# The first layer's weights in eight loads of 256 KB instead of sixteen of 128 KB, and a new order of all work

## The chip, the core and the metric

The kernel runs on one core of one Trainium2 chip. A core has a matrix engine (TensorE, PE in the profile; its weight loads are PEld), a vector engine (VectorE, DVE), a scalar engine (ScalarE, ACT), a general engine (GpSimd, POOL) and a queue engine (SyncE, SP). Each works through its own list of instructions in order; semaphores make one wait for another. DMA engines move data between the chip's main memory and the core's on-chip memory; a transfer is issued by an instruction of GpSimd, SyncE or ScalarE. The metric is the device time of one execution in microseconds (us); lower is better.

## What is computed

Eight batches of two softmax attentions in a row, then a two-layer network with a squared ReLU, all inputs and outputs in float32:

```python
def sm_attn(qq, kk, vv):
    s = scale * np.matmul(qq, kk.transpose(0, 1, 3, 2))
    s = s - np.max(s, axis=-1, keepdims=True)
    a = np.exp(s)
    a = a / (np.sum(a, axis=-1, keepdims=True) + 1e-09)
    return np.matmul(a, vv)
p_packed = sm_attn(p, k, v)
out = sm_attn(q, p_packed, p_packed)
...
h = x @ w_in
r = np.maximum(h, 0.0)
g = r * r
return (g @ w_out).astype(np.float32)
```

There are 8 batches, 8 heads, 576 queries and keys for each, heads of 64, and 32 packed queries p. After the attention the heads stand side by side, so that x has 4608 rows of 512; w_in is 512 x 2048 and w_out 2048 x 512.

## The kernel before

**Stages.** Batch by batch the kernel does the following; the names are those of its own list of work, with the batch as first number. `S1` multiplies packed queries with keys (L733; L749 for batches 5 to 7), `MX` takes the row maximum (L752), `EX` the exponential (L760), `E` turns the result round (L766, or a DMA transpose for batches 5 to 7), `PV` multiplies with the values (L780), `XN` divides by the sum, `XM` and `XC` turn that round (L799). `M` multiplies the result with w_in (L810): as the second attention is linear in its values, w_in is applied to the 32 packed rows of each head before the attention weights are. `MC` casts `M` from the accumulators to on-chip memory (L606 on ScalarE, L608 on VectorE). `S2` multiplies queries with the packed rows (L827, L837), `SI` turns the scores round on VectorE (L848), `SM` takes the maximum (L854), `SU` subtracts it (L858), `SE` is the exponential on ScalarE (L861), `SS` the sum (L864), `SN` divides (L871), `SO` turns the weights round (L875). `F` and `F1` multiply these weights with `M`, which gives the first layer (L912 for batches 0 and 1, L884 later), `R` is the ReLU (L920 and L922, L894 and L896), `Q` and `SQ` the square (L930 and L932, L902 and L904). `F2` is the second layer (L938), partly in groups that save one multiplication in eight (`GP`, L1005, fed by sums and differences `gS` on VectorE, L990). Results go out through L950.

**Batch 0 in thirds.** The first batch is cut into three parts of 128, 192 and 256 tokens, so that the first layer can start early: `F.0.0`, `F.0.1` and `F.0.2`, and `SE.0.0` to `SE.0.2` in the same way. w_in is used in four quarters of 512 columns, `M.0.0` to `M.0.3`; a quarter has to be there as a whole before its `M` is complete.

**Loads.** All loads but the first keys and p are issued by GpSimd (`load`, L1048) in a fixed order, `ORDER`: keys and values of batch 0, a first part of its queries, the first quarter of w_in, the rest of the queries, the other quarters, then keys of batch 1, w_out, and so on. They convert from float32 to bfloat16 on the way. A load waits until the load eight places before it has landed (`issued[-8]`), so at most eight are under way. A quarter of w_in came as four loads: two halves of the embedding (`qd`), each in two pairs of heads (`i`), 128 KB each in bfloat16.

**Order.** No engine's order is written by hand. A planner (`Plan.forward`) goes through time with a cost for each piece of work and picks by a priority: a level by batch and stage, plus a number for each piece from `TABLE`. The table was found by a search. The planner's costs and the landing times that it assumes decide which piece is put first; the program that comes out is fixed, and every engine then follows its list whatever the real times are. Where the planner expects TensorE to be idle for over 0.7 us, it puts in fills (`keep_clock`, L612), matmuls of a zero tile whose result nobody reads.

Of the kernel before, what the change touches and what calls it, by code (L numbers as in the profile page):

```python
# [14 lines left out]
P = 128  # L15
D = 64
# [5 lines left out]
WCH = 512  # L22
# [19 lines left out]
class Plan:  # L42
# [6 lines left out]
    def add(self, *a, **kw):  # L49
        self.pieces.append(Piece(*a, **kw))  # L50
# [177 lines left out]
TABLE = {'o': {'Lk.0.0i': -41.988702, 'Lk.0.1i': 172.502158, 'Lk.0.0': 181.505648, 'LP.0': -6.041854, 'Lk.0.1':  # L228
# [289 lines left out]
def kernel_impl(tc, q, k, v, p, w_in, w_out, out):  # L518
    nc = tc.nc
# [22 lines left out]
    with ExitStack() as ctx:  # L542
# [52 lines left out]
        QDS = range(NQD)  # L595
# [800 lines left out]
```

## Time and profile before

| | us |
|---|---|
| median of 3 runs | 235.95 (235.69 to 235.96) |
| profiled execution, its own time | 235.75 |
| its span, first to last instruction | 234.0 |
| TensorE busy | 221.4 (95%) |
| VectorE busy | 198.1 (85%) |
| ScalarE busy | 152.0 (65%) |
| GpSimd busy | 59.9 (26%) |

The granted TensorE clock was 0.995 of full speed over the span. A row of a group reads: line, engine, operation, output and input with their shapes, count, then busy time, mean ns of one, and the idle time of the engine just before them with what ended it. A row of the timeline reads: start and length in us, engine, line, what it is, count, and in brackets the idle time before it with its releaser. In the chain of waits each row is a start, a length and what the time went to. A row of a stretch reads: from and to, length, busy time and count for each engine, granted clock, share of the DMA engines, GB/s. Busy times of matmuls are modelled and overlap, so that eight matmuls of 0.27 us each can take 0.87 us together.

### The profile page before, as it was taken

Reading aid. Unit: us, or ns where it says so; the run is one execution under the profiler, and the core shown is the slowest. Engines: PE = TensorE matmul, PEld = TensorE weight load, DVE = VectorE, ACT = ScalarE, POOL = GpSimd, SP = SyncE. Lnnn points to the kernel's source line nnn. Section 1 sums busy time; section 2 is a strip of 40 time slices with the busy share of each in tenths; the row PEclk is TensorE's granted clock in tenths of the full one; section 3 lists DMA queues with packets and bytes.
Section 4 is the critical chain, followed back from the end, with each engine's and each line's share of the span. In section 5 each row is a group of like instructions: output and inputs, shape, how many; then the busy total and the mean of one; then the engine's idle time right before and its main releaser. Section 6 shows DMA issues by size and latency. Waiting matters only on the chain.

```text
span 234.0 us, 6384 instructions
## 1 busy us (share of the span) xinstructions
PE 221.4 (95%) x2621; PEld 159.9 (68%) x2638; DVE 198.1 (85%) x332; ACT 152.0 (65%) x247; POOL 59.9 (26%) x107
## 2 busy tenths in 40 slices
PE   8878899999999999999999999999999999999991
PEld 5655665346554566678768787877777888888781
DVE  3769887799999988999999789999999999877240
ACT  3333897469875799984999846459985998501100
POOL 9777745233343666620000000000000000000000
PEclk9999999999999999999999999999999999999998
DMA  7999999999999999999788689609710023205316
GB/s 235 179 169 175 195 204 204 204 194 250 240 205 241 227 220 177 174 182 125 175 150 135 134 116 191 140 2 204 134 39 8 4 44 73 65 0 112 70 43 181
DMA packets 46716, 34.06 MB, mean 146 GB/s; under 512 B 25376, under 2 KB 38432, under 8 KB 46688
## 3 DMA queue, kind: packets, MB, share of 16 engines
q0 software_dynamic: 19456, 18.03, 48.8%
q1 hardware_dynamic: 26304, 14.98, 29.8%
q10 hardware_dynamic: 928, 0.66, 0.9%
q8 instruction: 20, 0.33, 0.6%
q14 instruction: 8, 0.07, 0.1%
HBM read 37.22 MB, written 9.44 MB: 199 GB/s over the span
## 4 chain that ended last, share of the span: by engine, by line
PE 77%; DMA 14%; DVE 3%; POOL 1%; issue 1%; SPq 1%; ACT 0%; DVEq 0%; POOLq 0%
PE ps L1005 29%; PE ps L884 20%; PE ps L938 13%; DMA kq_b<-in_q_dram 7%; PE ps L912 5%; PE ps L810 3%; DMA w_in_b<-in_moe_w_in_dram 3%; DMA v_b<-in_v_dram 3%; DMA out_dram<-o_sb 2%; PE ps L956 1%; PE ps L780 1%; PE ps L827 1%; SPq L950 1%; PE ps L733 1%; POOL v_b L621 1%
## 5 line engine op out<-in xcount | busy, mean ns | idle before, releaser
L894 ACT ACTIVATE r_b<-ps 128x576 bf16<-128x576 f32 x92 | 52.8, 662 | 8.5 <-PE ps L884 8.3
L884 PE MATMUL ps<-a,M 128*128 128x288 bf16 x384 | 52.5, 286 | 0.2
L884 PEld LDWEIGHTS <-M 128*128 128x128 bf16 x384 | 37.3, 98 | 11.6 <-DVE a L875 0.2
L938 PE MATMUL ps<-w_out_b,gT 128*128 128x512 bf16 x159 | 41.2, 380 | 1.3 <-issue 0.6
L1005 PEld LDWEIGHTS <-gT 128*128 128x128 bf16 x384 | 36.9, 98 | 7.5 <-issue 2.4
L606 ACT CAST M<-ps 128x1024 bf16<-128x1024 f32 (+1 forms) x33 | 29.8, 940 | 10.9 <-PE ps L810 8.7
L904 DVE TENSOR_TENSOR gT<-r_b 128x1152 bf16<-128x1152 bf16 x40 | 29.3, 745 | 4.0 <-ACT r_b L894 3.7
L606 ACT COPY o_sb<-ps 128x512 f32<-128x512 f32 (+1 forms) x21 | 11.9, 575 | 30.5 <-PE ps L1005 16.6
L950 POOL DMA_DIRECT2D out_dram<-o_sb x2 | 1.1, 570 | 119.2 <-DVE o_sb L1025 117.7
L1005 PEld LDWEIGHTS <-gS 128*128 128x128 bf16 x288 | 27.7, 98 | 5.1 <-issue 1.8
L938 PEld LDWEIGHTS <-gT 128*128 128x128 bf16 x176 | 15.8, 98 | 15.3 <-issue 2.5
L1025 DVE TENSOR_TENSOR o_sb<-o_sb,ps 128x512 f32<-128x512 f32 x30 | 20.3, 676 | 6.5 <-PE ps L1005 5.7
L1005 PE MATMUL ps<-wS,gT 128*128 128x256 bf16 x192 | 23.5, 273 | 0.5 <-DVE o_sb L1025 0.5
L1005 PE MATMUL ps<-w_out_b,gT 128*128 128x256 bf16 x192 | 23.8, 273 | 0.0
L1005 PE MATMUL ps<-wS,gS 128*128 128x256 bf16 x192 | 23.5, 273 | 0.0
L920 ACT ACTIVATE r_b<-ps 128x512 bf16<-128x512 f32 (+2 forms) x25 | 15.7, 664 | 7.7 <-PE ps L912 6.4
L912 PE MATMUL ps<-a,M 128*128 128x256 bf16 (+3 forms) x160 | 18.6, 262 | 1.3 <-DVE M L608 0.8
L912 PEld LDWEIGHTS <-M 128*128 128x128 bf16 x160 | 13.8, 98 | 6.4 <-issue 1.1
L760 ACT ACTIVATE e<-ps,n 128x576 bf16<-128x576 f32 x16 | 11.7, 737 | 7.0 <-DVE n L752 6.8
L612 PE MATMUL ps<-o_sb 128*128 128x256 bf16 x97 | 14.6, 311 | 1.1 <-DVE o_sb L615 1.1
L752 DVE TENSOR_REDUCE n<-ps 128x1 f32<-128x576 f32 x16 | 11.6, 750 | 2.0 <-PE ps L733 1.8
L612 PEld LDWEIGHTS <-o_sb 128*128 128x128 bf16 x97 | 10.2, 111 | 4.4 <-DVE o_sb L615 1.1
(77 smaller groups left out, 316.9 us busy)
## 6 DMA issues: line engine op xcount, KB each, us to landing
out_dram<-o_sb SPq DMA_DIRECT2D x65, 128.0 KB, 3.4
kq_b<-in_k_dram POOLq DMA_DIRECT2D x14, 288.0 KB, 10.9
kq_b<-in_q_dram POOLq DMA_DIRECT2D x10, 288.0 KB, 6.9
w_in_b<-in_moe_w_in_dram POOLq DMA_DIRECT2D x16, 128.0 KB, 6.1
w_out_b<-in_moe_w_out_dram POOLq DMA_DIRECT2D x8, 256.0 KB, 9.4
v_b<-in_v_dram POOLq DMA_DIRECT2D x5, 320.0 KB, 11.4
v_b<-in_v_dram POOLq DMA_DIRECT2D x12, 128.0 KB, 7.7
v_b<-in_v_dram POOLq DMA_DIRECT2D x5, 256.0 KB, 9.8
```

The source lines that it names most:

```text
L606: nc.scalar.copy(dst, src)
L612: nc.tensor.matmul(half(7)[:, :2 * P], lhsT=zero[:, :P], rhs=zero, start=True, stop=True)
L752: nc.vector.tensor_reduce(n1[b % 2][:, qd:qd + 1], ps1[b, qd], axis=AX.XY if b in XBAR else AX.X, op=ALU.max, negate=True)
L760: nc.scalar.activation(e_out(qd) if b in XBAR else e1[:, qd, :S], ps1[b, qd], ACT.Exp, bias=n1[b % 2][:, qd:qd + 1], accum_out=d1[b % 2][: ...
L884: nc.tensor.matmul(t[:, c], lhsT=M[b % 2][:, qd, fb * FB:(fb + 1) * FB], rhs=a2[b % 2][:, qd, c * HALF:(c + 1) * HALF], start=(qd == 0), s ...
L894: nc.scalar.activation(dst, src, ACT.Relu)
L904: eng.tensor_tensor(out=dst, in0=r, in1=r, op=ALU.mult)
L912: nc.tensor.matmul(t[:, c, m * w:(m + 1) * w], lhsT=M[b % 2][:, qd, fb * FB:(fb + 1) * FB], rhs=a2[b % 2][:, qd, o:o + w], start=(qd == 0) ...
L920: nc.scalar.activation(dst, ph["h", b, x, j], ACT.Relu)
L938: nc.tensor.matmul(po[t], lhsT=gT[:, fb, n0:n0 + P], rhs=w_out_b[:, fb, :], start=(fb == 0), stop=(fb == NFB - 1))
L1005: nc.tensor.matmul(pz[g, k][:, i], lhsT=a[:, f, i * P:(i + 1) * P], rhs=w[:, f], start=(k not in ON and h == 0 and f == 0 and i == 0), sto ...
L1025: nc.vector.tensor_tensor(out=oC(g, i, j), in0=oC(g, *src), in1=pz[g, z], op=ALU.add)
```

## The change

A quarter of w_in comes as two loads (one for each half of the embedding, all four heads) instead of four. The order of the bytes in `ORDER` is the same. The planner's figures for these loads are changed to match, it assumes that some of the early loads land 0.8 us later than before, and the table of priorities is replaced as a whole by that of a new search (837 numbers for the order before, 821 after). `M` waits for two loads instead of four. Nothing else is changed; the arithmetic is the same.

```diff
-        def dma_w_in(c, i, qd):
+        def dma_w_in(c, qd):
             src = w_in[:, c * WCH:(c + 1) * WCH].rearrange("(qd h d) f -> qd d h f", qd=NQD, h=QH)
-            nc.gpsimd.dma_start(w_in_b[qd * D:(qd + 1) * D, 2 * i:2 * i + 2, c * WCH:(c + 1) * WCH], src[qd][:, 2 * i:2 * i + 2])
+            nc.gpsimd.dma_start(w_in_b[qd * D:(qd + 1) * D, :, c * WCH:(c + 1) * WCH], src[qd])
...
-            add(name, [("DMA", us, None)], [f"{name}i"], line="dma", lag=0.9, level=-200)
+            late = 0.8 * (name[:3] == "LWO" or name.split(".")[:2] in (["LWI", "1"], ["LWI", "2"], ["LWI", "3"]) or name[:2] != "LW" and name.split(".")[1] in "12")
+            add(name, [("DMA", us, None)], [f"{name}i"], line="dma", lag=0.9 + late, level=-200)
...
-                for i in range(2):
-                    for qd in QDS:
-                        load(f"LWI.{n}.{i}.{qd}", 0.7 + 0.45 * ((n, i, qd) in ((1, 0, 0), (3, 0, 0), (3, 1, 1))), lambda n=n, i=i, qd=qd: dma_w_in(n, i, qd), 0.6)
+                for qd in QDS:
+                    load(f"LWI.{n}.{qd}", 1.35, lambda n=n, qd=qd: dma_w_in(n, qd), 0.73)
...
-                add(f"M.{b}.{c}", [("PE", 0.216, lambda u, b=b, c=c: m_mm(b, c, u))], [f"XC.{b}"] + [f"LWI.{c}.{i}.{qd}" for i in range(2) for qd in QDS]
+                add(f"M.{b}.{c}", [("PE", 0.216, lambda u, b=b, c=c: m_mm(b, c, u))], [f"XC.{b}"] + [f"LWI.{c}.{qd}" for qd in QDS]
```

What this does to the engines' lists: GpSimd has 100 instructions instead of 107 in the listing. TensorE has 98 fills instead of 97, and the same matmuls otherwise. In the third quarter's turn ScalarE's list now has `SE.0.2` ahead of the two casts of `M.0.2`; before it stood between them. Two pieces of `F.0.2` stand behind batch 1's `S1` instead of ahead of it. The scores `S1.7` of the last batch stand closer behind `S1.6`. The ends of the lists, from the last pieces of the first layer on, differ little.

More of the change, by code (lines that the diff above doesn't have):

```diff
@@ L226 @@
 XTURN = (5, 6, 7)
-TABLE = {'o': {'Lk.0.0i': -41.988702, 'Lk.0.1i': 172.502158, 'Lk.0.0': 181.505648, 'LP.0': -6.041854, 'Lk.0.1':
[287 rows of a table removed]
+TABLE = {'o': {'Lk.0.0i': -1.867589, 'Lk.0.1i': 4.847526, 'Lk.0.0': 27.298004, 'LP.0': 2.29922, 'Lk.0.1': 26.572586,
[282 rows of a table added]
 def kernel_impl(tc, q, k, v, p, w_in, w_out, out):
```

569 rows, old and new, of the table TABLE are left out of this document.

## The prediction

> **What bounds the kernel now.** I read the page first, then the busy time in stretches, then the chain of waits, then the first 33 us instruction by instruction.
>
> ```profile
> PE 221.4 (95%) x2621; PEld 159.9 (68%) x2638; DVE 198.1 (85%) x332; ACT 152.0 (65%) x247; POOL 59.9 (26%) x107
> ```
>
> TensorE is the busy engine. Cut at the first scores of batch 1 (31.90) and the last matmul (229.2), columns PE, PEld, DVE, ACT, POOL:
>
> ```profile
> 0.00:31.90 31.90, 26.49 (x333) 18.80 (x334) 22.83 (x56) 15.54 (x28) 23.94 (x45) 1.00 1.11 192
> 31.90:229.20 197.30, 194.96 (x2288) 141.14 (x2304) 175.30 (x277) 136.14 (x220) 35.86 (x63) 1.00 0.76 138
> ```
>
> ```profile
> L612 PE MATMUL ps<-o_sb 128*128 128x256 bf16 x97 | 14.6, 311 | 1.1 <-DVE o_sb L615 1.1
> ```
>
> After 31.90 TensorE idles 197.30 - 194.96 = 2.3 us. A new order can win at most that there, and lose more. The first stretch is different: all 97 fills of L612, matmuls that compute nothing, lie in its 26.5 us, and 31.90 - 26.49 = 5.4 us are idle. What the change is worth is decided before batch 1 starts. The chain of waits in that stretch runs through loads:
>
> ```profile
> 11.07 5.45 DMA kq_b<-in_q_dram
> 16.81 6.82 DMA w_in_b<-in_moe_w_in_dram
> ```
>
> The second is the last load of the third quarter of w_in (M.0.2 needs it), issued only when the queries of the first had landed. TensorE, ScalarE and VectorE around it:
>
> ```profile
> 22.52 0.40 PE L810 MATMUL ps<-w_in_b,ppT 64*32 64x512 bf16 x5
> 23.67 0.39 PE L810 MATMUL ps<-w_in_b,ppT 64*32 64x512 bf16 x3 [0.74 <-DMA w_in_b<-in_moe_w_in_dram]
> 24.99 2.14 PE L912 MATMUL ps<-a,M 128*128 128x192 bf16 x24
> 27.67 1.06 PE L912 MATMUL ps<-a,M 128*128 128x256 bf16 x8 [0.20 <-DVE a L875]
> 31.90 0.71 PE L733 MATMUL ps<-kT,pT 32*32 32x512 bf16 x32 [0.22 <-DVE r_b L922]
> ```
>
> ```profile
> 22.63 0.60 ACT L920 ACTIVATE r_b<-ps 128x512 bf16<-128x512 f32 x1 [1.09 <-PE ps L912]
> 24.10 0.59 ACT L606 CAST M<-ps 128x512 bf16<-128x512 f32 x1 [0.87 <-PE ps L810]
> 24.58 0.63 ACT L861 ACTIVATE e<-s 128x512 bf16<-128x512 f32 x1
> ```
>
> ```profile
> 16.62 0.65 DVE L697 STREAM_TRANSPOSE qT<-kq_b 128x448 f32<-128x448 f32 x1 [0.64 <-DMA kq_b<-in_q_dram]
> 22.56 0.63 DVE L858 TENSOR_TENSOR s<-s,m 128x512 f32<-128x512 f32 x1
> 23.97 0.37 DVE L875 STREAM_TRANSPOSE a<-n 128x192 f32<-128x192 f32 x1
> 25.25 0.69 DVE L864 TENSOR_REDUCE t<-e 128x16 f32<-128x512 bf16 x1 [0.91 <-ACT e L861]
> 27.17 0.45 DVE L875 STREAM_TRANSPOSE a<-n 128x256 f32<-128x256 f32 x1
> 27.54 0.98 DVE L932 TENSOR_TENSOR gT<-r_b 128x768 bf16<-128x768 bf16 x2
> 29.73 0.85 DVE L932 TENSOR_TENSOR gT<-r_b 128x512 bf16<-128x512 bf16 x2
> 31.20 0.65 DVE L922 TENSOR_SCALAR r_b<-ps 128x512 bf16<-128x512 f32 x1
> ```
>
> See how one late load travels: M.0.2 stands 0.74; its cast stands in ScalarE's queue ahead of the exponential of the last third of batch 0 (SE.0.2); that exponential's input was ready at 22.56 + 0.63 = 23.19, yet it starts at 24.58; VectorE then stands 0.91, and F.0.2, the last third of the first layer, opens at 27.67.
>
> **The change part by part.** Loads first.
>
> ```profile
> L688 POOL DMA_DIRECT2D w_in_b<-in_moe_w_in_dram x16 | 9.5, 622 | 2.5 <-DMA kq_b<-in_q_dram 1.0 <-DMA w_in_b<-in_moe_w_in_dram 0.7 <-DMA v_b<-in_v_dram 0.6
> L691 POOL DMA_DIRECT2D w_out_b<-in_moe_w_out_dram x8 | 5.7, 713 | 4.8 <-DMA w_out_b<-in_moe_w_out_dram 1.8 <-DMA v_b<-in_v_dram 1.6 <-DMA w_in_b<-in_moe_w_in_dram 1.2
> ```
>
> A 256 KB load of w_in has no row; L691 is one of that size and 2 KB pieces, so I take 713 ns. GpSimd saves 16 x 0.622 - 8 x 0.713 = 4.2 us of issuing. By itself this is worth 0: POOL is 26% busy and waits for landings. If the issue cost a full 2 x 0.622, nothing is saved, which is still 0.
>
> What moves the path is the window: a load waits for the one eight loads before it.
>
> ```profile
> 5.42 1.82 POOL L688 DMA_DIRECT2D w_in_b<-in_moe_w_in_dram  x3
> 9.98 0.58 POOL L654 DMA_DIRECT2D kq_b<-in_q_dram  x1 [1.02 <-DMA v_b<-in_v_dram]
> 11.57 4.21 POOL L688 DMA_DIRECT2D w_in_b<-in_moe_w_in_dram  x7
> 16.81 0.58 POOL L688 DMA_DIRECT2D w_in_b<-in_moe_w_in_dram  x1 [1.02 <-DMA kq_b<-in_q_dram]
> ```
>
> ```profile
> w_in_b<-in_moe_w_in_dram POOLq DMA_DIRECT2D x16, 128.0 KB, 6.1
> ```
>
> Eight loads of double size are more bytes in flight. In the new order the last load of the third quarter waits for the first load of the first quarter, whose second half was issued at 5.42 + 0.61 and lands about 6.1 later, at 12.1; so it is issued near 12.7 in place of 16.81. When it lands is then set by bytes. Behind the last piece of the queries (11.07 + 5.45 = 16.52) stand two quarters, 4 x 256 KB = 1.05 MB, at the rates of
>
> ```profile
> 18.00:24.00 6.00, 4.62 (x54) 3.01 (x52) 5.96 (x17) 2.09 (x4) 4.24 (x8) 1.00 1.17 173
> 24.00:30.00 6.00, 5.35 (x60) 4.44 (x58) 4.89 (x12) 5.71 (x10) 4.37 (x7) 1.00 1.17 200
> ```
>
> 173 to 200 GB/s: 5.2 to 6.1 us, so 21.7 to 22.6. The bounds are 21.7 and 23.63 (16.81 + 6.82, no gain, if one slow DMA engine and not the window set it). I take 22.4, nearer to the bytes, because the old load was issued after GpSimd had stood 1.02 for the window. The wait of 0.74 goes. The keys of batch 1 and w_out are issued earlier too, but stand in the same queue of bytes behind the weights; I give that 0.
>
> Five of M.0.2's eight matmuls ran ahead of the last small load, 0.40 us in all; with large loads they would stand behind it if that still came last. The Trainium skill, "Perfetto Trace Analysis", section "DMA Optimizations", has a rule against this change: splitting DMAs into smaller chunks may let some work start sooner. By that rule the trace agrees for these five, and the sum below would come out 0.4 higher; by the landing times above they wait for nothing.
>
> The order. In the new one SE.0.2 stands ahead of both casts of M.0.2 on ScalarE. It starts when its input and the relu before it are done, at about 23.2 (22.63 + 0.60), 1.4 us earlier than 24.58. VectorE's sum at 25.25 follows by 1.4; the transposition at 23.97, which used to lie in VectorE's idle time, now comes behind that sum and gives back 0.3. The two casts, 0.59 each, now end near 25.0; the F that needs them stands behind ten fills and starts about then, as the F in that place did (24.99). F.0.2 can open at 27.67 - 1.4 + 0.3 = 26.6. From there to S1.1, the first scores of batch 1, it was 31.90 - 27.67 = 4.23, nearly all VectorE work. The new list there has one square of 768 columns less (0.98 / 2), one of 512 less (0.85 / 2) and a relu of 768 columns in place of 512 (half of 0.65 more): 4.23 - 0.49 - 0.42 + 0.33 = 3.65. S1.1 comes at 30.25, so 1.65 earlier. But less is done by then: two pieces of F.0.2, eight matmuls, moved behind S1.1, and one matmul more of F2 ahead of it.
>
> ```profile
> 35.83 0.87 PE ps L912 x8
> 36.70 0.65 PE ps L938 x3
> ```
>
> That is 0.87 - 0.22 = 0.65 us of work still owed. Net 1.65 - 0.65 = 1.0 us. There are 98 fills in place of 97; the extra one lies in idle time, or costs 0.1.
>
> Behind S1.1 the matmuls, stores and the last 56 + 16 of TensorE are the same in kind and number, in another order. The old order lost 2.3 us there; nothing says that the new one loses the same. I take a loss of 0.2, with ends of -1 (under half of the 2.3 idle) and +1.2 (the third rival below).
>
> Sum, against the profiled run of 235.75 (span 234.0 and 1.75 around it): -1.0 + 0.1 + 0.2 = -0.7, 235.05. The median of the runs, 235.95, stands 0.2 above the profiled one, so 235.2 for the median.
>
> **The rivals.**
>
> Queries come earlier too. The first of the three last pieces of q waited for the values (1.02 at 9.98); in the new order it waits for nothing, and the last is issued at about 10.0 in place of 11.07. If they land earlier by the 0.64 that VectorE stands at 16.62, the whole softmax of batch 0 shifts: 235.2 - 0.64 = 234.6. For it: those waits were for the window. Against: the same bytes stand ahead of them.
>
> The loads land as before. Then M.0.2 still ends near 24.0, ten fills (at most 14.6 / 97 = 0.15 each; I take 1.1) follow it in TensorE's order, and the first F that needs its casts starts at 25.1 to 25.7; the fourth quarter and the relus behind it shift by about 0.6 to 0.7, and 0.3 is left of the 1.0: 235.2 + 0.65 = 235.85. The rows from 18 to 30 speak for it: the DMA share is 1.17, so a longer queue may win nothing. This is also the case in which the change in loads does not do what it says.
>
> VectorE is overrun by batches 6 and 7. S1.7 came 149.28 - 134.44 = 14.8 us after S1.6; in the new order 20 matmuls of L884, 32 of L1005 and some 1.2 us of small ones lie between, 2.48 + 3.60 + 1.2 = 7.3 us, so half.
>
> ```profile
> 128.75 2.48 PE ps L884 x20
> 134.44 0.38 PE ps L749 x26
> 135.27 3.60 PE ps L1005 x32
> 149.28 0.38 PE ps L749 x26
> ```
>
> ```profile
> 138.00:144.00 6.00, 5.68 (x9) 1.00 1.09 214
> 144.00:150.00 6.00, 6.00 (x10) 1.00 0.72 160
> ```
>
> ```profile
> L752 DVE TENSOR_REDUCE n<-ps 128x1 f32<-128x576 f32 x16 | 11.6, 750 | 2.0 <-PE ps L733 1.8
> ```
>
> VectorE (the columns are its busy time, the clock, the DMA share, GB/s) is full there: 0.32 us free in 12. Batch 7's two maxima of 0.75 move in, ahead of the differences (gS) that release the groups of L1005: 1.5 - 0.3 = 1.2 us. From the point where VectorE is behind TensorE's stock of released groups, each microsecond is idle TensorE: 235.2 + 1.2 = 236.4, and more with the small work that follows the maxima. Against it: the same work is then missing from 150 on, and TensorE showed no idle in 138 to 150.
>
> **How the numbers follow.** Forecast 0.33, queries earlier 0.17, loads as before 0.22, VectorE overrun 0.28. The likeliest gives 235.2. Its own range is 234.8 to 235.7; for 8 in 10 I reach from 233.9 (queries earlier and 0.7 won behind S1.1) to 236.9 (the overrun, and 0.5 for the small work behind the maxima). About 0.2%, 0.47 us, is what can be told from no change here. Faster by more (below 235.48): 0.27 of the forecast, the queries' 0.17, 0.04 of the third, 0.48 in all. Within 0.2%: 0.06 and 0.18, 0.24. Slower: 0.28.
>
> **What would show it.** Right: the wait of M.0.2 for w_in is gone or under 0.2; SE.0.2 starts near 23.2 and ends ahead of the casts; VectorE's wait of 0.91 is gone; the first L733 of batch 1 starts between 29.8 and 30.8; TensorE's idle time from there to its last matmul is 2 to 3 us. Wrong: M.0.2 waits until 23.6 or later; S1.1 is at 31 or later; or TensorE idles over 4 us behind S1.1, with VectorE named at L1005 between 140 and 165.

## The result, and the profile after

| | before | after |
|---|---|---|
| median of four runs each, us | 235.82 (235.34 to 235.96) | 237.59 (236.8 to 237.8) |
| ratio, 95% interval | | 1.0087 (1.0062 to 1.0113) |
| profiled execution, its own time / span, us | 235.75 / 234.0 | 237.58 / 235.8 |

The changed kernel is 1.8 us slower. That lies outside of the range, and on the other side of the forecast.

The page after: busy time, and the same two stretches as before, cut at the first scores of batch 1 (S1.1), now at 31.19:

```profile
PE 223.3 (95%) x2626; PEld 160.8 (68%) x2639; DVE 202.6 (86%) x336; ACT 150.7 (64%) x243; POOL 55.3 (23%) x99
```

```profile
0.00:31.19 31.19, 26.15 (x327) 18.21 (x328) 22.21 (x54) 15.19 (x27) 19.78 (x38) 0.95 1.14 204
31.19:230.70 199.51, 197.11 (x2300) 142.62 (x2312) 180.38 (x284) 135.11 (x216) 35.36 (x62) 1.00 0.78 135
```

The first stretch is 0.71 us shorter (31.90 - 31.19), the second 2.2 longer (199.51 - 197.30). TensorE's idle time in the second is 199.51 - 197.11 = 2.4 us, as before (2.3). These two numbers can't be compared as they stand, because both traces lack records of matmuls. The second layer's line has 176 weight loads in each kernel, but only 159 matmuls in the trace of before and 163 in that of after; a place where one is missing is drawn as idle. Before:

```profile
L938 PE MATMUL ps<-w_out_b,gT 128*128 128x512 bf16 x159 | 41.2, 380 | 1.3 <-issue 0.6 <-DMA kq_b<-in_q_dram 0.2 <-ACT r_b L920 0.2
L938 PEld LDWEIGHTS <-gT 128*128 128x128 bf16 x176 | 15.8, 98 | 15.3 <-issue 2.5 <-DVE gT L932 0.2
```

Two runs of the experiments below have all their records: bf, the old order with ten more fills in its front, and e0, the kernel after once more. The same stretch (S1.1 to the last matmul) of bf, then of e0:

```profile
31.30:227.98 196.68, 196.67 (x2305) 141.17 (x2304) 175.27 (x277) 136.11 (x219) 35.95 (x63) 1.00 0.78 138
```

```profile
31.18:230.78 199.60, 197.95 (x2313) 142.61 (x2312) 180.38 (x284) 135.17 (x216) 35.82 (x63) 1.00 0.77 135
```

The old order leaves TensorE 0.01 us idle there, the new one 1.65, and all but 0.2 of that waits for VectorE. In the trace of before 0.54 of the 2.3 is a wait (for VectorE, at 218 us), and the rest is missing records. VectorE has 180.38 us of work in the second stretch in place of 175.30.

TensorE, VectorE and ScalarE in the front of the changed kernel:

```profile
14.69 3.18 PE L607 MATMUL ps<-o_sb 128*128 128x256 bf16 x15
17.80 0.59 PE L822 MATMUL ps<-qT,pq 32*32 32x192 bf16 x32
22.72 0.41 PE L805 MATMUL ps<-w_in_b,ppT 64*32 64x512 bf16 x8
31.19 0.70 PE L728 MATMUL ps<-kT,pT 32*32 32x512 bf16 x32
```

```profile
16.77 0.65 DVE L692 STREAM_TRANSPOSE qT<-kq_b 128x448 f32<-128x448 f32 x1 [0.60 <-DMA kq_b<-in_q_dram]
...
26.66 0.45 DVE L870 STREAM_TRANSPOSE a<-n 128x256 f32<-128x256 f32 x1 [0.64 <-PE ps L907]
```

```profile
23.41 0.63 ACT L856 ACTIVATE e<-s 128x512 bf16<-128x512 f32 x1
23.95 1.05 ACT L601 CAST M<-ps 128x512 bf16<-128x512 f32 x2
```

M.0.2 runs its eight matmuls at 22.72 without a wait, and SE.0.2 starts at 23.41 ahead of the two casts. But S1.1 comes only 0.71 us earlier, not 1.65. One reason is S2.0.1, the scores of the second third of batch 0: most of its matmuls start at 17.80, before at 17.31. TensorE, before:

```profile
17.31 0.58 PE L827 MATMUL ps<-qT,pq 32*32 32x192 bf16 x28 [0.72 <-DVE qT L697]
```

The queries that S2.0.1 needs still land late (16.77, before 16.62), although their last piece was issued at 10.21 (before 11.07), and the 15 fills that start at 14.69 run until 17.8, though the transposition of the queries has ended at 16.77 + 0.65 = 17.42. The landings of the queries, before and then after (median us from issue in the last column):

```profile
kq_b<-in_q_dram POOLq DMA_DIRECT2D x1, 224.0 KB, 4.3
kq_b<-in_q_dram POOLq DMA_DIRECT2D x2, 112.0 KB, 4.9
```

```profile
w_in_b<-in_moe_w_in_dram POOLq DMA_DIRECT2D x8, 256.0 KB, 8.1
kq_b<-in_q_dram POOLq DMA_DIRECT2D x1, 224.0 KB, 8.5
kq_b<-in_q_dram POOLq DMA_DIRECT2D x2, 112.0 KB, 6.8
```

The chain of waits, shares by engine, before and then after:

```profile
PE 77%; DMA 14%; DVE 3%; POOL 1%; issue 1%; SPq 1%; ACT 0%; DVEq 0%; POOLq 0%
```

```profile
PE 58%; DVE 21%; DMA 9%; issue 4%; ACT 3%; POOL 2%; SPq 1%; DVEq 0%; ACTq 0%; POOLq 0%
```

VectorE has 21% of it in place of 3%: on the page of after, this is where the loss shows.

**Where the time goes.** To find the places I compared when two kernels have done the same useful work. Each matmul of TensorE's list counts the time from its start to the next one's in back-to-back rows of the profile before (0.2165 us for one of F2, 0.1226 for one of 288 columns, 0.1092 in the groups), a fill counts nothing, and the table gives how much later (+) or earlier (-) than the profiled run before each kernel reaches the sum that the old one had reached at the time on the left. Each column is one execution.

| old kernel's time | after | e0 (after again) | e3 | g41 | h41n | x1 |
|---|---|---|---|---|---|---|
| 32.0 | -0.20 | -0.20 | -1.27 | -0.20 | -1.49 | -1.39 |
| 42.4 | -0.19 | -0.18 | -1.24 | -0.26 | -1.47 | -1.37 |
| 51.0 | -0.84 | -0.85 | -1.90 | -0.54 | -0.39 | -2.03 |
| 59.0 | +0.22 | +0.05 | -1.02 | +0.09 | -0.39 | +0.09 |
| 81.2 | -0.01 | -0.01 | -1.01 | +0.03 | -0.30 | -0.13 |
| 105.9 | +0.98 | +0.98 | -0.07 | +1.02 | -0.30 | +0.73 |
| 142.2 | +1.15 | +1.15 | +0.10 | +1.19 | | +0.90 |
| 150.3 | +1.55 | +1.50 | +0.45 | +1.57 | -0.23 | +1.34 |
| 166.5 | +1.73 | +1.67 | +0.63 | +1.39 | -0.24 | +1.51 |
| 202.9 | +1.72 | +1.68 | +0.60 | +1.36 | -0.24 | +1.45 |

The changed kernel wins 0.2 by 32 us and 0.6 more by 51 (second-layer work done ahead), and then loses 1.06 at 51 to 59, 1.0 at 81 to 106, 0.4 at 142 to 150 and some 0.2 up to 166. The table ends ahead of one more wait, at 218, of 0.54 in before and 0.55 in e0, which other runs of both orders lack or have shorter (bf 0, e3 0.29). TensorE in the first two of these places, after:

```profile
50.54 1.04 PE L907 MATMUL ps<-a,M 128*128 128x256 bf16 x8
...
55.71 0.27 PE L907 MATMUL ps<-a,M 128*128 128x256 bf16 x1
56.27 1.36 PE L907 MATMUL ps<-a,M 128*128 128x256 bf16 x11 [0.29 <-DVE a L870]
...
83.95 1.14 PE L879 MATMUL ps<-a,M 128*128 128x288 bf16 x8 [0.33 <-DVE a L870]
```

The first layer of batch 1 opens at 50.54 as before (50.52); the first matmul of its second part (320 columns) starts at 58.33, before at 57.97. Both waits name L870, the transposition of the attention weights (SO) on VectorE. What VectorE got: relus and squares, before and then after.

```profile
L904 DVE TENSOR_TENSOR gT<-r_b 128x1152 bf16<-128x1152 bf16 x40 | 29.3, 745 | 4.0 <-ACT r_b L894 3.7
L902 ACT ACTIVATE gT<-r_b 128x1152 bf16<-128x1152 bf16 x8 | 9.4, 1179 | 0.2
L896 DVE TENSOR_SCALAR r_b<-ps 128x576 bf16<-128x576 f32 x4 | 3.0, 752 | 0.0
```

```profile
L899 DVE TENSOR_TENSOR gT<-r_b 128x1152 bf16<-128x1152 bf16 x34 | 25.0, 747 | 2.3 <-ACT r_b L889 2.1
L897 ACT ACTIVATE gT<-r_b 128x1152 bf16<-128x1152 bf16 x14 | 16.5, 1176 | 0.1
L891 DVE TENSOR_SCALAR r_b<-ps 128x576 bf16<-128x576 f32 x12 | 8.8, 741 | 1.1 <-PE ps L879 0.7 <-DVE s L853 0.3
```

Eight relus moved to VectorE and six squares away from it.

### The profile page after: what moved, and what is told of

Same layout as the page of the kernel before. It is cut to its first block, busy times and chain, and to the rows that moved or that the text cites. A ratio compares the mean times of both kernels' runs of the same rounds, so it can differ in the third digit from the quotient of the medians.

```text
span 235.8 us, 6385 instructions
## 1 busy us (share of the span) xinstructions
PE 223.3 (95%) x2626; PEld 160.8 (68%) x2639; DVE 202.6 (86%) x336; ACT 150.7 (64%) x243; POOL 55.3 (23%) x99
## 4 chain that ended last, share of the span: by engine, by line
PE 58%; DVE 21%; DMA 9%; issue 4%; ACT 3%; POOL 2%; SPq 1%; DVEq 0%; ACTq 0%; POOLq 0%
PE ps L1000 21%; PE ps L879 17%; PE ps L933 9%; DMA kq_b<-in_k_dram 4%; PE ps L907 4%; DMA w_in_b<-in_moe_w_in_dram 3%; DVE o_sb L1020 2%; DVE gS L985 2%; DVE m L849 2%; PE ps L805 2%; DVE s L853 2%; DMA out_dram<-o_sb 2%; DVE t L859 2%; PE ps L951 1%; DVE gT L899 1%
## 5 line engine op out<-in xcount | busy, mean ns | idle before, releaser
L889 ACT ACTIVATE r_b<-ps 128x576 bf16<-128x576 f32 x84 | 49.4, 662 | 16.1 <-PE ps L879 15.9
L1000 PEld LDWEIGHTS <-gT 128*128 128x128 bf16 x384 | 36.9, 98 | 7.3 <-issue 2.4
L601 ACT COPY o_sb<-ps 128x512 f32<-128x512 f32 (+1 forms) x19 | 10.9, 577 | 32.1 <-PE ps L1000 17.7
L601 ACT CAST M<-ps 128x1024 bf16<-128x1024 f32 (+1 forms) x31 | 27.7, 936 | 5.7 <-PE ps L805 5.7
L933 PEld LDWEIGHTS <-gT 128*128 128x128 bf16 x176 | 16.4, 98 | 15.9 <-issue 1.5
L899 DVE TENSOR_TENSOR gT<-r_b 128x1152 bf16<-128x1152 bf16 x34 | 25.0, 747 | 2.3 <-ACT r_b L889 2.1
L915 ACT ACTIVATE r_b<-ps 128x512 bf16<-128x512 f32 (+2 forms) x23 | 14.4, 653 | 9.1 <-PE ps L907 8.8
L897 ACT ACTIVATE gT<-r_b 128x1152 bf16<-128x1152 bf16 x14 | 16.5, 1176 | 0.1
```

Of the source, the lines that this page charges most:

```text
L601: nc.scalar.copy(dst, src)
L889: nc.scalar.activation(dst, src, ACT.Relu)
L897: nc.scalar.activation(dst, r, ACT.Square)
L899: eng.tensor_tensor(out=dst, in0=r, in1=r, op=ALU.mult)
L915: nc.scalar.activation(dst, ph["h", b, x, j], ACT.Relu)
L933: nc.tensor.matmul(po[t], lhsT=gT[:, fb, n0:n0 + P], rhs=w_out_b[:, fb, :], start=(fb == 0), stop=(fb == NFB - 1))
```

## The experiments

Ratios stand against runs of the kernel before on the same chip, with the 95% interval.

| run | what | median us (runs) | ratio |
|---|---|---|---|
| e0 | after, again | 237.33 (12) | 1.0062 (1.0040 to 1.0084) |
| e1 | old order, large loads | 235.25 (12) | 1.0001 (0.9981 to 1.0021) |
| e2 | new order, small loads | 238.52 (5) | 1.0146 (1.0116 to 1.0176) |
| e3 | after, ten more fills | 236.34 (7) | 1.0059 (1.0035 to 1.0082) |
| e4 | after, two casts early | 237.43 (6) | 1.0100 (1.0070 to 1.0130) |
| e5 | after, relus and squares on their old engines | 238.84 (6) | 1.0146 (1.0115 to 1.0177) |
| e6 | e1, softmax ahead of casts | 234.87 (12) | 0.9978 (0.9956 to 0.9999) |
| e7 | e4, more moved back | 238.05 (6) | 1.0099 (1.0071 to 1.0127) |
| h30 | new order to 30 us, old behind | 236.66 (9; a tenth took 454.6) | 1.0042 (1.0012 to 1.0072) |
| h30f | the same with ten fills | 236.94 (6) | 1.0063 (1.0042 to 1.0084) |
| h41n | new to 41 us, old behind | 236.26 (12) | 1.0028 (1.0006 to 1.0051) |
| h41f | the same with ten fills | 235.82 (12) | 0.9999 (0.9978 to 1.0019) |
| h49 | new to 49 us, old behind | 239.04 (6) | 1.0164 (1.0140 to 1.0188) |
| h82 | new to 82 us, old behind | 238.11 (6) | 1.0105 (1.0077 to 1.0132) |
| g41 | old to 41 us, new behind | 236.85 (10) | 1.0063 (1.0038 to 1.0087) |
| bf | before, ten more fills | 234.95 (12) | 0.9974 (0.9955 to 0.9994) |
| x1 | e3, two waits taken away | 237.71 (6) | 1.0121 (1.0078 to 1.0164) |
| y1 | e6 and bf together | 234.92 (12) | 0.9974 (0.9953 to 0.9994) |

**The loads, and the order.** e1 has the old order with the large loads: the first of each pair of issues brings both pairs of heads, the second nothing.

```diff
-            nc.gpsimd.dma_start(w_in_b[qd * D:(qd + 1) * D, 2 * i:2 * i + 2, c * WCH:(c + 1) * WCH], src[qd][:, 2 * i:2 * i + 2])
+            if i == 0:
+                nc.gpsimd.dma_start(w_in_b[qd * D:(qd + 1) * D, :, c * WCH:(c + 1) * WCH], src[qd])
```

> The old order of all work, with the eight loads of 256 KB in place of the sixteen. Theory A (the loss of 1.8 us comes from the new order, the loads alone help): the last load of the third quarter lands by 23, TensorE's wait of 0.74 ahead of L810 is gone, and nothing behind the first scores of batch 1 changes: 235.2 to 235.8. Theory B (the larger loads themselves cost, by what they push back in the queue of bytes): 236.5 to 237.6, with a DMA named in a wait of TensorE or VectorE that the old kernel does not have.

e2 is the reverse: the new order, each load of 256 KB issued as two of 128.

```diff
-            nc.gpsimd.dma_start(w_in_b[qd * D:(qd + 1) * D, :, c * WCH:(c + 1) * WCH], src[qd])
+            for i in range(2):
+                nc.gpsimd.dma_start(w_in_b[qd * D:(qd + 1) * D, 2 * i:2 * i + 2, c * WCH:(c + 1) * WCH], src[qd][:, 2 * i:2 * i + 2])
```

> The new order of all work, each load of 256 KB issued as two of 128 KB at the same place. Theory A: 237.2 to 238.3, as slow as the changed kernel or slower, and M.0.2 waits for w_in again by up to 0.7. Theory B: 235.5 to 236.2.

The loads alone are worth nothing (1.0001). In e1 M.0.2 runs without a wait too, but the queries come later, so S1.1 is at 31.67. VectorE and TensorE of e1:

```profile
16.97 0.65 DVE L698 STREAM_TRANSPOSE qT<-kq_b 128x448 f32<-128x448 f32 x1 [1.47 <-DMA kq_b<-in_q_dram]
```

```profile
22.88 0.41 PE L811 MATMUL ps<-w_in_b,ppT 64*32 64x512 bf16 x8
```

The order carries the loss, and with small loads it is slower still. There GpSimd builds an identity matrix behind more issues, and TensorE waits for it at 11.20 (after: the same matmuls at 9.19 without a wait). TensorE of e2:

```profile
11.20 0.44 PE L762 MATMUL ps<-ident,e 128*128 128x128 bf16 x5 [1.50 <-POOL ident masks.py:199]
23.71 0.39 PE L806 MATMUL ps<-w_in_b,ppT 64*32 64x512 bf16 x3 [0.55 <-DMA w_in_b<-in_moe_w_in_dram]
```

**The clock.** The profiled run after shows a granted clock of 0.95 in the first stretch: the 15 fills above took 3.18 us, 0.21 each, and S2.0.1 stood behind them. e0 is the same kernel once more; e3 adds ten fills where TensorE idles just before.

```diff
+MORE = {'PV.0': 3, 'XM.0': 4, 'M.0.0': 3}
...
+            seq.append([p, n + MORE.get(p.name, 0)])
```

> The changed kernel as it is, beside the others on one chip: 1.8 us slower than the old one by the record, 1.0 if the 3.4 us at half clock do not come on this chip. The runs with a granted clock of 0.997 or more should be 0.7 to 1.1 faster than those with less.

> The changed kernel with ten more fills between 11.5 and 14.2 us (3 ahead of the values product, 4 ahead of the transposition, 3 ahead of the first quarter of batch 0), where TensorE has its idle time just ahead of the 3.4 us at half clock. Theory C (the half clock follows a stretch of light work, and costs 0.8): the granted clock is 0.997 or more in the runs and the median is 236.6 to 237.0. Rival (the dip comes whatever stands there, or costs nothing on the path): clock 0.993 in most runs and 237.4 to 237.9.

e0's trace has the full clock from 12 to 18 us (1.00, after 0.72), yet S2.0.1 at 17.84, S1.1 at 31.18 and the table's curve as after. So a full clock doesn't take the loss away. The two traces agree in S1.1 for different reasons: in after the slow fills held S2.0.1 by some 0.4, in e0 the queries landed 0.4 later. Nor are e0's runs at a clock of 0.997 or more (237.23 to 237.99) faster than its others, though the expectation had them 0.7 to 1.1 faster. In e3's trace the queries came early and S1.1 at 30.12; its ratio isn't told apart from e0's. VectorE of e0, then of e3:

```profile
17.14 0.65 DVE L692 STREAM_TRANSPOSE qT<-kq_b 128x448 f32<-128x448 f32 x1 [0.83 <-DMA kq_b<-in_q_dram]
```

```profile
16.05 0.63 DVE L710 STREAM_TRANSPOSE qT<-kq_b 128x448 f32<-128x448 f32 x1
```

TensorE of e0, then of e3:

```profile
17.84 0.58 PE L822 MATMUL ps<-qT,pq 32*32 32x192 bf16 x28 [1.36 <-DVE qT L692]
```

```profile
16.73 0.59 PE L840 MATMUL ps<-qT,pq 32*32 32x192 bf16 x32
```

S1.1 comes 13.3 to 13.4 us behind these matmuls in after, e0 and e3, and 14.6 behind them in before.

In the traces of kernels with the large loads the queries land early or late. Early (that transposition at 15.7 to 16.05, no wait) were e3, e5, h30f, h41n and x1; late (16.5 to 17.2) after, e0, e4, e7, h30, h41f, h49, h82, g41, and e1, e6, y1. h41n and h41f differ by ten fills alone, and there the one without is early; in after and e3 it is the one with. Each is one execution, so whether the kernel decides it or the execution stays open too.

**Repairs of the new order.** These edits take the planner's finished list and move pieces ahead of others (`MOVES`: piece, and the one it is put ahead of), or change an engine (`SWAP`). e4 puts the last two quarters of batch 1's `M`, and their casts, back to where the old order had them, at 43 to 48 us.

```diff
+MOVES = [('M.1.2', 'F2.3.10'), ('MC.1.2', 'SE.1.0'), ('M.1.3', 'F2.0.12'), ('MC.1.3', 'FC.2')]
```

> The changed kernel with the third and fourth quarter of batch 1's first-layer weights (M.1.2, M.1.3) and their two casts put back to 43 to 48 us, where the old order had them and ScalarE is idle, in place of 53 to 56.5. Theory D (those two casts, 1.9 us of ScalarE in the stretch where the first layer of batch 1 lives on ScalarE and VectorE, make the loss of 1.3 us between 51 and 60): 236.2 to 236.7. Rival (VectorE paces that stretch, with the softmax of batch 1 and the sums wS, and the casts are beside it): 237.2 to 237.7.

e5 gives 28 relus and squares of batches 2 to 7 the engine that they had before.

```diff
+SWAP = {'R.2.0': 'ACT', 'R.2.6': 'ACT', 'SQ.3.0': 'ACT', 'SQ.3.1': 'DVE',
...
```

> The changed kernel with 28 relus and squares of batches 2 to 7 given back to the engine that had them in the old one (13 relus from VectorE to ScalarE or the other way, 15 squares likewise), in the new order of all work otherwise. A relu of 576 columns takes 0.59 on ScalarE and 0.73 on VectorE, a square of 1152 columns 1.18 on ScalarE and 0.73 on VectorE; the new list has 8 more relus on VectorE and 6 more squares on ScalarE, 3.8 us more work for the same result. Theory W (that is what TensorE waits for behind 80 us, where both engines are full): 0.5 to 1.0 less than the changed kernel run beside it, and VectorE's busy time 199 to 201 in place of 202.6. Rival (the positions in the order decide, not the engine): within 0.3 of it, or slower.

e7 is e4 with `WS.2.1` (sums of w_out on VectorE) and a transposition of batch 2's keys behind `SO.1.0`, and six pieces of F2 spread through the first layer.

```diff
+MOVES = [('M.1.2', 'F2.3.10'), ('MC.1.2', 'SE.1.0'), ('M.1.3', 'F2.0.12'), ('MC.1.3', 'FC.2'), ('F2.1.10', 'F.1.0.2'), ('F2.1.11', 'F.1.0.2'), ('F2.1.12', 'F.1.0.3'), ('F2.1.13', 'F.1.0.3'), ('F2.1.14', 'F2.5.0'), ('F2.1.15', 'F2.5.0'), ('FC.1', 'Q.1.0.3'), ('ST.1', 'Q.1.0.3'), ('WS.2.1', 'Tk.2.1'), ('Tk.2.0', 'Tk.2.1')]
```

> The changed kernel with the two casts moved as in e4 and, on VectorE, a sum of w_out (WS.2.1) and a transposition of queries (Tk.2.0), 1.4 us, put behind the last softmax step of batch 1's first half, so that its first layer (F.1.0.0, at 50.5) can open at 49.2, with the last six matmuls of F2.1 spread between its matmuls. Theory S (TensorE is ahead of the old kernel by 0.8 at 51 us, but by matmuls of F2 taken from stock, and gives it back at 51 to 59, where VectorE's softmax and relus set the pace): F.1.0.0 at 49.0 to 49.6, the loss of 1.1 between 51 and 59 falls to 0.4 or less, and the time is 0.5 to 1.0 less than the changed kernel's. Rival (VectorE's sum of work up to 60 us sets it, whatever stands first): F.1.0.0 comes early, but the time is within 0.3.

None helps, and e5 is worse: TensorE now waits for relus. So giving the relus and squares back, in the new positions, does not win the time back. VectorE's busy time falls from 202.6 to 201.2 only (before 198.1), so e5 doesn't settle whether the sum of VectorE's work is. In e7 the first layer of batch 1 opens at 50.45 and not at 49.2, so the edit did not do what it was made for, and neither of its theories was tried. In e4 the second wait of batch 1's first layer is longer than after (0.52, after 0.29). TensorE of e4:

```profile
55.90 0.27 PE L925 MATMUL ps<-a,M 128*128 128x256 bf16 x1
56.69 1.36 PE L925 MATMUL ps<-a,M 128*128 128x256 bf16 x11 [0.52 <-DVE a L888]
```

**One order up to a time, the other behind.** In these kernels the planner is replaced by a list written out: the pieces that one order starts before a time, with their engines, then the rest in the other's.

```diff
-        for p in sorted(out, key=lambda p: p.start):
+        for name, e, units, n in SEQ:
+            p = at[name]
...
```

> The new order up to the first scores of batch 1 (every piece of work but F2 that the new list has ahead of them), the old list from there on for all that is left, with the old engines and banks; eight loads of 256 KB. Theory O (the front of the new order wins 1.1, or 0.2 where 3.4 us of it run at half clock, and the order behind it loses 2.5): 234.1 to 235.1, and TensorE keeps to the end the lead over the old kernel that it has at 35 us. Rival Y (whatever the front wins, VectorE's chain of batch 1 gives it back in any order): within 0.3 of the old kernel, the lead gone by 60 us.

> The same, with the ten more fills of e3 between 11.5 and 14.2 us. Theory O with C (the fills keep the clock up): 233.9 to 234.4, 1.0 to 1.4 under the old kernel, with less spread than the same without fills. Rival Y: within 0.3 of the old kernel.

> The new order up to the opening of batch 1's first layer (49 us), the old list from there on. TensorE is 0.8 ahead of the old kernel there in the changed kernel. Theory O1 (the loss of 1.1 between 51 and 59 belongs to the list of that stretch): with the old list the lead stays, 234.4 to 235.0. Theory O2 (it was decided before 49 us: the F2 matmuls taken from stock at 43 to 50 and the two quarters of batch 1 still to come): the lead is gone by 60 here too, 235.2 to 235.9.

> The new order up to 82 us (the opening of batch 2's first layer), the old list from there on. The changed kernel is level with the old one there. Theory O (the other 1.7 us, at 81 to 106, 142 to 150 and 160 to 175, belong to the new list behind 82): 235.2 to 235.8, level with the old kernel. Rival: what is late at 82 (VectorE's softmax of batch 2, which ends 0.7 later) costs the same in any list: 235.8 to 236.4.

> The new order up to batch 1's second scores (S2.1, 41 us), with the ten more fills of e3, the old list from there on. h30f lost 2 us at its seam (it runs old pieces of F.0.2 ahead of batch 1's scores) and held its place to 0.1 from there to the end; here both lists have done the same work at the seam. Theory O (the old list behind keeps what the front wins): 1.0 to 1.4 under the old kernel run beside it. Rival Y (a lead cannot be held, VectorE's chain takes it back): within 0.3 of it.

> The same without the ten more fills. With theory C (3.4 us at half clock cost 1.1 here in the runs that have them): runs between 0.1 and 1.2 under the old kernel, the median 0.3 to 0.9 above that of the kernel with fills. Rival (the fills do nothing): the same median as with fills, within 0.2.

> The inverse: the old order up to batch 1's second scores, the new list from there on, eight loads of 256 KB. Theory N1 (the new list behind 41 us loses 1.6 to 1.8 by itself, at 51 to 59, 81 to 106, 142 to 150 and 160 to 175): 1.3 to 2.0 over the old kernel. Theory N2 (it only gives back a lead that it came with): within 0.5 of the old kernel.

With the old list behind, the offset that is there after the seam stays within 0.15 us up to 203 us: +2.47 in h30, +0.50 in h30f, +1.06 in h41f, -0.30 in h41n, +3.53 in h49, +2.30 in h82 (the seams at 49 and 82 us cost 4.4 and 2.3 by themselves, so these two say nothing of the new order's own stretch). h30f was over 1 us ahead at 30 us and lost it at its seam, where S1.1 waits 1.04 for VectorE and comes at 32.40. So the old list loses nothing from 51 us on, but none of these kernels beats before: Theory O forecast 1.0 to 1.4 under it for h41f, which is level (0.9999), and h41n is slower (1.0028). Their traces are of one execution each, h41n's the fastest of its twelve and h41f's one of its slower ones (236.2). With the new list behind, g41 loses in the same places as after, with the old front ahead of it (the table: +0.6 at 51 to 59, +1.0 at 81 to 106, +0.4 at 142 to 150), and its ratio is that of e0; the time is 1.3 us over the old kernel's, as Theory N1 had it. This shows that the loss behind 51 us belongs to the list behind batch 1's second scores, whatever front it follows. The shares of the chain of waits, g41 and then h41n:

```profile
PE 68%; DVE 18%; DMA 7%; issue 2%; POOL 1%; SPq 1%; ACT 0%; DVEq 0%; ACTq 0%; POOLq 0%
```

```profile
PE 79%; DVE 8%; DMA 5%; POOL 2%; ACT 1%; issue 1%; SPq 1%; DVEq 0%; POOLq 0%
```

It is so throughout: VectorE has 12 to 21% of the chain in every kernel with the new list in its second part (after, e0, e2 to e5, e7, g41, x1), and 2 to 8% in every one with the old.

h41n also shows what a lead is worth. It is 1.47 us ahead at 42 us, and 0.39 at 51. TensorE of h41n:

```profile
41.25 0.70 PE L1854 MATMUL ps<-qT,pq 32*32 32x256 bf16 x32
50.22 1.05 PE L1939 MATMUL ps<-a,M 128*128 128x256 bf16 x8 [0.63 <-DVE a L1902]
```

The second scores start 0.30 ahead of before (41.55), the first layer 0.30 (50.52): between them lies VectorE's softmax, 9.0 us in both. TensorE's lead was second-layer work done early, and it ran out of such work.

**Two waits taken away.** In the new list the second matmul of the piece `F.1.0.4` waits for the transposition `SO.1.1`, though it reads another part of that tile; in the old list `SO.1.1` stands behind those matmuls. x1 is e3 with three pieces written ahead of `SO.1.1`, so that this wait goes and `SO.1.1` waits for those matmuls instead, and with two transpositions of batch 3's queries behind `SO.2`.

```diff
+MOVES = [('F.1.0.4', 'SO.1.1'), ('F.1.0.5', 'SO.1.1'), ('F.1.0.6', 'SO.1.1'), ('Tq.3.0', 'R.2.0'), ('Tq.3.1', 'R.2.0'), ('Lk.6.1i', 'R.2.0')]
```

> The changed kernel with the ten more fills of e3, and the two waits taken away that the trace shows on VectorE. First: three matmul groups of batch 1's first layer (F.1.0.4 to 6) are written down ahead of SO.1.1, the transposition of the other half of the same tile, and no longer behind it; no engine's own order changes, only that the second matmul of F.1.0.4 does not wait for that transposition any more. Second: the two transpositions of batch 3's queries (Tq.3, 0.73 and 0.76) stand behind batch 2's last softmax step and no longer inside it. Theory V (the new list loses by single waits for VectorE, and each that goes is kept): the 0.44 in the F group at 55.7 goes, the 0.50 ahead of batch 2's first layer at 83.5 goes, and the time is 0.6 to 1.0 less than e3's, 0.0 to 0.5 over the old kernel. Rival (VectorE's sum of work sets the pace, so the waits come back behind): both waits go, and the time is within 0.3 of e3's, 1.0 to 1.6 over the old kernel.

Both waits go, and x1 is no faster than e3, from which it is made, and rather slower (1.0121, e3 1.0059). TensorE, then VectorE of x1:

```profile
54.50 1.49 PE L925 MATMUL ps<-a,M 128*128 128x256 bf16 x12
55.83 0.59 PE L951 MATMUL ps<-w_out_b,gT 128*128 128x512 bf16 x2
57.77 1.68 PE L925 MATMUL ps<-a,M 128*128 128x256 bf16 x12 [1.34 <-DVE r_b L935]
```

```profile
56.03 0.51 DVE L888 STREAM_TRANSPOSE a<-n 128x320 f32<-128x320 f32 x1 [1.45 <-PE ps L925]
...
57.03 0.68 DVE L935 TENSOR_SCALAR r_b<-ps 128x512 bf16<-128x512 f32 x1
```

Now `SO.1.1` waits 1.45 for those matmuls, the relu stands behind it in VectorE's queue (57.03), and TensorE waits 1.34 for that relu. From 51 to 59 us x1 loses 2.1, e3 0.9; from 81 to 106 it loses 0.86, e3 0.94, so 0.1 us is left of the second wait. The time is 2.3 over that of before in the runs beside it, more than either theory forecast. In the first place the wait taken from TensorE came back by way of VectorE's queue. That VectorE's order sets the pace in these places is argued from this, from the waits and from the shares of the chain; no repair won, so it is not shown.

**Better than both?** e6, bf and y1 keep the old order: e6 has the large loads and the exponentials of batch 0's second and third part ahead of a cast; bf only ten more fills; y1 both.

```diff
+MORE = {'PV.0': 3, 'XM.0': 4, 'M.0.0': 3}
+MOVES = [('SE.0.1', 'MC.0.1.1'), ('SE.0.2', 'MC.0.2.0')]
```

> The old order with eight loads of 256 KB, and two things of the new order's front alone: on ScalarE the exponentials SE.0.1 and SE.0.2 stand ahead of the casts of M.0.1 and M.0.2. My account of the front (loads and exponentials ahead of the casts together bring the first scores of batch 1 forward): they start at 30.5 to 31.2 in place of 31.9, and the time is 0.4 to 1.0 less than the old kernel's. Rival (what the front wins is lost at the opening of batch 1's first layer, which VectorE sets): the same scores come early, and the time is within 0.3 of the old kernel's.

> The old kernel, sixteen loads, with the ten more fills of e3 alone. Theory C: no run under a granted clock of 0.995, the median 0.0 to 0.4 under the old kernel's, because the slowest of its runs (clock 0.990 to 0.992) go. Rival (fills only fill): within 0.1, with the same spread.

> The old order with eight loads of 256 KB, SE.0.1 and SE.0.2 ahead of their casts (as e6) and the ten more fills (as bf). e6 and bf were each 0.2% under the old kernel. If they add up: 0.7 to 1.3 under the old kernel run beside it. Rival (both are the same gain, a front that is a little early, or none): 0.0 to 0.6 under it.

All three are 0.2 to 0.3% under before, with intervals that end just below 1; the gains don't add. In e6 S1.1 is at 31.66, so the exponential's place by itself doesn't bring the scores forward. bf still has four runs at a clock of 0.994, which Theory C had excluded. Where the half microsecond comes from stays open: up to 203 us bf's trace is ahead of before's by about 0.5 us and y1's by nothing, and their ratios are the same. All three traces lack the wait of 0.54 at 218 us that before's has, where VectorE stands 0.82 for a store to land; so does e1's, whose ratio is 1.0001.

## Why the prediction was wrong

*The issue saving is worth 0.* Right in the old order (e1). In the new one it isn't: with twice the issues the identity comes late, and S1.1 stood at 31.23 even so; how much of e2's loss hangs on that wasn't separated.

*The wait of M.0.2 goes, the landing near 22.4.* Right: 22.72 without a wait.

*SE.0.2 near 23.2, ahead of the casts.* Right: 23.41, and VectorE's wait of 0.91 is gone.

*S1.1 at 30.25, 1.0 net.* Half right. With early queries it was 30.12 (e3) and the lead at 32 us 1.27; in after and e0, where they landed late, 31.19 and 0.20. Two terms were off. The gain of the front was put at 1.65; S1.1 follows S2.0.1 by 13.4 us in place of 14.6, which is 1.2. The transposition ahead of F.0.2 waits 0.64 for matmuls of TensorE at 26.66, which the sum did not have, and F.0.2 opens at 29.06, not at 26.6. And S2.0.1 itself starts 0.5 later than before in after and e0. I had kept the queries' landing where it was, with earlier as a rival; the larger loads around them made it longer (6.8 us in place of 4.9), and in after the slow fills held S2.0.1 besides. Together these cost 0.8 of the 1.0.

*A loss of 0.2 behind S1.1, ends -1 and +1.2.* This step failed, and with it the forecast: counted from 32 us, the loss was 1.9 (from -0.20 to +1.72). It read TensorE's 2.3 us of idle time as something that the old order lost and a new one might win. But 1.7 of that was records missing from the trace: the old order leaves 0.01 us idle there in bf, so there was next to nothing to win. "The same in kind and number, in another order ... nothing says that the new one loses the same" put the new list's own waits at almost nothing without a look at them. What was there to see in the two lists is eight more relus on VectorE at 0.74 us and six squares fewer at 0.75, and a cast of batch 1's `M` on VectorE at 41.08; in all VectorE has 5.1 us more work in the stretch. In place of 0.2 the runs show that the new list behind batch 1's second scores loses 1.6 behind the old front (g41, from -0.26 to +1.36) and 1.9 behind its own, where the old list loses nothing from 51 us on. Which of VectorE's pieces is to blame they don't show.

*The third rival, VectorE overrun.* The right engine in the wrong place. It was to cost 1.2 us at S1.7, behind 138; there it cost 0.4. Most lies at 51 to 59 and 81 to 106, where batches 1 and 2 open their first layers. I had read only the stretch in which S1.7 moved. At 51 to 60 the old list keeps its offset to 0.1 us with VectorE 95% busy (8.53 of 9.00 us, row below), so there was no room there for more. Before, then after:

```profile
51.00:60.00 9.00, 8.95 (x62) 5.84 (x61) 8.53 (x18) 8.03 (x15) 2.87 (x5) 1.00 1.14 249
```

```profile
51.00:60.00 9.00, 8.42 (x69) 5.06 (x69) 8.58 (x19) 7.58 (x13) 3.40 (x6) 1.00 1.16 256
```

VectorE works as long in both; in after TensorE and ScalarE do less beside it, TensorE by half a microsecond.

*The signs to look for.* Idle TensorE of 2 to 3 us was to show the step right. It was 2.4, and the loss was there all the same: with 17 records missing before and 13 after, the sign could not tell the 0.54 that TensorE really waits in before from the 1.65 of e0.

The Trainium skill's rule on splitting loads ("Perfetto Trace Analysis", section "DMA Optimizations"), which I had weighed for M.0.2, did not show there: its five early matmuls waited for nothing. With the small loads, in e2, its last three stood 0.55.

Open: what of the 1.9 is not drawn as idle (in e0 1.1 of it is, up to 203 us); which order of VectorE's pieces costs the time at 51 to 59 and 81 to 106 (no single repair, e4, e5, e7 or x1, won it back); the losses at 142 to 166 were not tried by themselves.

## What to carry to other kernels

When a search replaces the order of a program with one busy engine and a second close behind, cost the second engine's queue in every stage, not only where the list visibly moved: here nearly all that TensorE waited for behind the front was a VectorE that was 86% busy. Before idle time is read as room to win, compare the number of matmuls with that of weight loads: 17 missing records looked like 1.7 us of slack. Compare two orders at equal useful work, which shows the place of a loss. A front that gains by early loads is worth only what the stage behind it can use, and only in runs in which the loads do land early.

## What was not expected of the hardware

Small loads took longer to land among larger ones. In the traces of the three kernels with loads of 128 KB (before, bf, e2) the queries' pieces of 112 KB landed 4.8 to 5.6 us after their issue and that of 224 KB 4.3 to 4.5; in those of the 17 with loads of 256 KB it was 6.3 to 7.8 and 7.0 to 8.9. With the larger loads the transposition that needs the last piece started at 15.7 to 16.05 or at 16.5 to 17.2, and kernels that differ in nothing near it fell on both sides (h30 late, h41n early).

In the profiled run of the kernel after 15 fills in a row took 0.21 us each (3.18 in all; granted clock 0.95 over the first stretch, 0.72 from 12 to 18 us), as in that of h82. In the next profiled run of the same kernel (e0) the clock stayed at full there, and the times were the same (237.58 and 237.5): the queries landed 0.4 later in it, and S2.0.1 started at 17.80 and 17.84.
